# Batch 0 of a windowed attention with FFN: exponentials as weights, outputs turned by TensorE, parts of 372 and 396 queries

## The chip, the cores and the metric

One core of a Trainium2 chip runs one launch. The metric is the device time of that launch in microseconds; three runs of the kernel before gave 254.47, 255.00 and 255.22, median 255.0. The engines have short names in what follows: PE is TensorE, DVE is VectorE, ACT is ScalarE, POOL is GpSimd and SP is SyncE. SP, ACT and POOL can issue transfers (DMA); POOL's are the ones that change the type on the way.

## The reference

Attention over 4 batches of 8 heads, 768 positions, 64 channels per head. A query sees the last 128 positions up to itself, and the first four positions ("sinks") always. Its output, laid out as 3072 tokens by 512 channels, goes through an FFN whose gate is a ReLU, with 1536 inner channels.

```python
keep = is_sink | in_window                    # key < 4, or 0 <= query - key < 128
scores = where(keep, q @ k.T / sqrt(64), -1e9)
a = exp(scores - max(scores)); a = a / (sum(a) + 1e-9)
x = (a @ v) as (batch * seq, head * dim)
out = (maximum(x @ w_gate, 0) * (x @ w_val)) @ w_out
```

## The kernel before, in words

**Units.** Attention is done in 16 units of two heads each: unit i is head pair i % 4 of batch i // 4. For a unit, keys lie in a tile `kE` and queries in `qT`, both turned so that the channels are on the partitions (two heads on 128), with extra key tiles in `kE` that begin with copies of the four sinks. Sg computes a group of score tiles on PE into one of two PSUM pairs (`PP`), and ACT takes exponentials from there into `ee`. DVE multiplies masks in; for two groups of batch 0 the mask is added on PE beforehand, as a bias.

**Two ways from exponentials to the FFN's input.** For batch 0, V multiplies `ee` by `v` with queries along the columns, so that the output is already turned: a sum over ones gives the denominators, spread over 64 partitions, DVE turns them, takes reciprocals and turns them back (R), and one more DVE instruction writes `xT`. It runs in two parts of 384 queries. For batches 1 to 3, W takes slices of 128 columns of `ee` as weights and streams 65 columns of `v`, whose last column is 1 and gives the denominators; queries then lie on partitions in seven tiles (`QSEG`), and DVE normalises them into `xn`. For batch 1, X turns `xn` on PE and ACT copies the result into `xT`; for batches 2 and 3 the turn goes through DRAM.

**FFN.** `chunk(b, g, m)` is column tile m (128 inner channels, 12 of them) of half g of batch b's queries: four matmuls with `wg`, a ReLU on ACT, four matmuls with `wv`, and a product on DVE into `hT`. In PSUM it rotates through three of four banks G; the fourth is for turns and for output tiles. `ffn2` multiplies `hT` by `wo` and stores 128 rows per tile.

**Order.** The program is written out by hand. After a head that brings up the first half of batch 0, 96 slots follow, one chunk each: 24 for a batch, for batch 0 first its twelve tiles of g = 0, then those of g = 1. `prep[s]` is what is emitted ahead of the chunk of slot s (loads, casts and stores, mostly on SP and POOL), and `plan[s]` what comes after it on PE: H and T turn halves and wholes of k and q, S is a score group, V, W and X are as above, F an output matmul. From slot 24 on three output matmuls follow each slot; those left over come at the end.

**Queues.** Each engine takes its instructions in the order emitted. On SP: loads of k, q and v, stores and turns by transfer, and the output. On POOL: casts from float32 (k and q into `kn` and `qn`, v into `vn`) and between them the issues of the weight loads, `load_w`, for two column tiles at a time, 256 KB each for `wg` and `wv`. In the kernel before, `prep[1]` holds them in this order:

```python
prep[1] += [("half", 6), ("half", 7), ("w", 6, 8), ("v", 0, 3), ("v", 0, 4), ("w", 8, 10), ("v", 0, 5),
            ("v", 0, 6), ("w", 10, 12)]
```

`setup3` fills the ends of `ee` and the ones beside v, on POOL; it stands in `prep[7]`. `gate(u)` is a small write by ACT into a load's buffer; the loads of units 4 to 6, in `prep[8]`, follow it, and so they start when ACT gets there. The loads of `v` for batch 0 use row tiles 0 to 2 in the head and 3 to 6 after it.

Of the kernel before, what the change touches and what calls it, by code (L numbers as in the profile page):

```python
# [15 lines left out]
CUT = 384  # L16


@with_exitstack
def kernel(  # L20
# [12 lines left out]
    nc = tc.nc  # L33
# [8 lines left out]
    NR, PR = 12, 64  # L42
# [4 lines left out]
    npool = ctx.enter_context(tc.tile_pool(name="np", bufs=2))  # L47
# [22 lines left out]
    ones = const.tile([128, 64], BF16, name="ones")  # L70
# [4 lines left out]
    m0 = const.tile([128, 512], BF16, name="m0")  # L75
# [12 lines left out]

# [3 lines left out]
           3: (1, 0, 152, [(244, 244, 0, 140), (ODD + 136, 372, 140, 152)]),  # L92
           4: (1, 152, 507, [(244, 384, 152, 267), (ODD + 136, 384, 267, 507)]),
           5: (0, 0, 499, [(0, 0, 0, 247), (ODD, 120, 247, 499)])}

    VLAST = [(4, 2, 0, 252, 112), (6, 2, 252, 272, 364), (5, 2, 272, 416, 240), (4, 2, 416, 419, 364)]
    VSEG = [[(0, 0, 0, 247, 0), (1, 0, 247, 499, 120), (2, 1, 0, 140, 244), (3, 1, 140, 152, 372)],
            [(2, 1, 152, 267, 0), (3, 1, 267, 507, 0)] + VLAST]
# [5 lines left out]

    class Unit:
# [4 lines left out]

    def load_kq(u):
        for x, dst in ((k, kf[u.i % NQ]), (q, qf[u.i % NQ])):
            nc.sync.dma_start(out=dst[:], in_=x[u.b, 2 * u.p:2 * u.p + 2].rearrange("h (p n) d -> (h p) (n d)", n=NR))
# [31 lines left out]
    def cast_kq(u):  # L145
        for src, dst in ((kf[u.i % NQ], kn[u.i % 2]), (qf[u.i % NQ], qn[u.i % 2])):
            nc.gpsimd.tensor_copy(dst[:], src[:])

# [23 lines left out]

    def load_rows(u):
        for x, dst in ((q, qf), (k, kf)):
            nc.sync.dma_start(out=dst[u.i % NQ][:].rearrange("p (h e) -> p h e", h=2),
                              in_=x[u.b, 2 * u.p:2 * u.p + 2].rearrange("h (p n) d -> p h (n d)", n=6))

    def cast_rows(u):
        for src, dst in ((qf, qn), (kf, kn)):
            nc.gpsimd.tensor_copy(dst[u.i % 2][:].rearrange("p (n h d) -> p h n d", n=6, h=2),  # L180
                                  src[u.i % NQ][:].rearrange("p (h n d) -> p h n d", n=6, h=2))

    def to_dram(u):
        for i, x in enumerate((qn, kn)):
            nc.sync.dma_start(out=kqd[u.i - ND][i * S:i * S + S, :].rearrange("(p n) c -> p (n c)", n=6),
                              in_=x[u.i % 2][:])
# [15 lines left out]
    def load_w(m0, m1):  # L202
        for w, dst in ((moe_w_gate, wg), (moe_w_val, wv)):
            nc.gpsimd.dma_start(out=dst[:, :, m0 * 128:m1 * 128],
                                in_=w.rearrange("(ko ki) n -> ki ko n", ki=128)[:, :, m0 * 128:m1 * 128])
# [5 lines left out]
    def setup():  # L211
# [9 lines left out]
        nc.gpsimd.affine_select(out=m0[:, 0:247], in_=band[:, 0:247], compare_op=Alu.is_ge, fill=0.0,  # L221
                                base=119, pattern=[[0, 247]], channel_multiplier=-1)
        cp, ms = nc.vector.tensor_copy, nc.vector.memset
        for i in range(NT):
            ms(kE[i][:, 384:1176], 0.0)
        ms(ones[:], 1.0)
        ms(vn[0][:, 3, :, 0:64], 0.0)
        ms(vf[:, 6, :, :], 0.0)
        cp(m0[:, 247:499], band[:, 4:256])
        ms(m0[0:4, 247:499], 1.0)  # L230
        ms(m0[0:4, 0:120], 1.0)
        ms(m0[0:4, 120:247], 0.0)
        bias(mb[:, 0, 0:499], m0[:, 0:499])
        bias(mb[:, 1, 0:140], band[:, 0:140])
        bias(mb[:, 1, 140:152], band[:, 4:16])
        ms(mb[0:4, 1, 140:152], 0.0)
# [4 lines left out]
    def setup2(g):  # L241
        cp, ms = nc.vector.tensor_copy, nc.vector.memset
        if g == 0:
            cp(msk[:, 0, 8:252], m0[:, 0:244])
            cp(msk[:, 0, 252:504], m0[:, 247:499])
            cp(msk[:, 0, 504:507], m0[:, 244:247])
            return
# [8 lines left out]
    rot, srot = [0], [0]  # L256
    head = [True]
# [4 lines left out]

    def two():
        if head[0]:
            srot[0] += 2
            return G[srot[0] % 4][:], G[(srot[0] + 1) % 4][:]
        x = pair()
        return x[:, 0, :], x[:, 1, :]
# [6 lines left out]
    def T(u):  # L275
        t = u.i % NT
        tk, tq = G[3][:], pair()[:, 0, :]
        for x, ps in ((kn[u.i % 2], tk), (qn[u.i % 2], tq)):
            for n in range(NR):
                for h in range(2):  # L280
                    r = slice(64 * h, 64 * h + 64)
                    nc.tensor.transpose(ps.bitcast(BF16)[r, 64 * n:64 * n + 64], x[r, 64 * n:64 * n + 64], ident[r, r])
        vk, vq = (ps.bitcast(BF16)[:, 0:S].rearrange("d (n p) -> d p n", p=PR) for ps in (tk, tq))
# [3 lines left out]
        nc.vector.tensor_copy(to(qT[t]), vq)  # L287
        odd_tiles(u, nc.vector.tensor_copy)

    def T_half(c):  # L290
        t, x = c % NP, c // NP
        if c < 2:
            tk, tq = two()
        elif head[0]:
            both = pair()
            tk, tq = both[:, 0, :], both[:, 1, :]
        else:
            tk, tq = G[3][:, 0:256], G[3][:, 256:512]
# [15 lines left out]
    def Sg(u, s):  # L314
        t, bias = u.i % NT, u.b == 0 and s in (0, 3)
        g, b0, n, segs = SEG[5 if u.b == 0 and s == 0 else s]
# [12 lines left out]
        if s == 4:  # L329
            parts = [(152, 267, band[:, 140:255]), (267, 507, msk[:, 1, 264:504])]  # L330
        else:
            parts = [] if bias else [(b0, n, msk[:, g, b0:n])]
        for c0, c1, m in parts:
            x = ee[u.i % NE][:, g, :, c0:c1]
            nc.vector.tensor_tensor(x, x, m.unsqueeze(1).to_broadcast([128, 2, c1 - c0]), op=Alu.mult)  # L335
# [3 lines left out]
    def sums(u, part, out, w):  # L339
        segs = VSEG[part]  # L340
        for i, (j, g, c0, c1, o0) in enumerate(segs):
            for h in range(2):
                nc.tensor.matmul(out=out[64 * h:64 * h + 64, o0:o0 + c1 - c0], lhsT=w(j, h),  # L343
                                 rhs=ee[u.i % NE][:, g, h, c0:c1], start=i == 0, stop=i == len(segs) - 1,
                                 skip_group_check=True)

    def V1(u, part):

        pv, pd = two()
        sums(u, part, pd, lambda j, h: ones[:])  # L350
        return u, part, pv, pd

    def V2(u, part, pv, pd):

        R = npool.tile([128, CUT], F32, name="R")
        r = npool.tile([128, CUT // 32], F32, name="r")
        nc.vector.transpose(out=R[:], in_=pd[:, 0:CUT])
        nc.vector.reciprocal(r[:], R[:].rearrange("p (c e) -> p c e", e=32)[:, :, 0])
        nc.vector.transpose(out=R[:].rearrange("p (c e) -> p c e", e=32),
                            in_=r[:].unsqueeze(2).to_broadcast([128, CUT // 32, 32]))  # L360
        return u, part, pv, R

    def V3(u, part, pv):
        sums(u, part, pv, lambda j, h: vn[u.b % 2][:, j, 2 * u.p + h, 0:64])

    def V4(u, part, pv, R):
        nc.vector.tensor_tensor(xT[u.b % 2][:, u.p, CUT * part:CUT * part + CUT], pv[:, 0:CUT], R[:], op=Alu.mult)  # L367
        ready[u.b, u.p, part] = True

    def V(u, part):  # L370
        x = V1(u, part)
        V3(*x[:3])
        V4(*V2(*x))

    def setup3():
        for i in range(2):
            nc.gpsimd.memset(vn[i][:, :, :, 64:66], 1.0)
        for i in range(NE):
            nc.gpsimd.memset(ee[i][:, 0:2, :, 507:640], 0.0)
            nc.gpsimd.memset(ee[i][:, 2, :, 419:640], 0.0)  # L380

    def W(u):

        ps = pair()
        for h in range(2):
            for t, segs in enumerate(QSEG):
                for i, (j, g, c0) in enumerate(segs):
                    nc.tensor.matmul(out=ps[:, h, 65 * t:65 * t + 65], lhsT=ee[u.i % NE][:, g, h, c0:c0 + 128],  # L388
                                     rhs=vn[u.b % 2][:, j, 2 * u.p + h, 0:65], start=t == 0 and i == 0,
                                     stop=t == 6 and i == len(segs) - 1, skip_group_check=True)  # L390
        o = ps[:, :, 0:455].rearrange("p h (t e) -> p h t e", e=65)
        x, r = xn[u.i % 2], rn[u.i % 2]
        nc.vector.reciprocal(r[:], o[:, :, :, 64])
        nc.vector.tensor_tensor(x[:].rearrange("p t (h d) -> p h t d", h=2), o[:, :, :, 0:64],  # L394
                                r[:].unsqueeze(3).to_broadcast([128, 2, 7, 64]), op=Alu.mult)

    def X(u):

        ps = (G[3][:] if u.p < 2 else pair()[:, 0, :]).bitcast(BF16)
        c = 0  # L400
        for t in range(7):
            nc.tensor.transpose(ps[:, c:c + 128], xn[u.i % 2][:, t, :], ident[:])
            c += 128 - t % 2 * 4
        nc.scalar.copy(xT[u.b % 2][:, u.p, :], ps[:, 8:8 + S])
        for x in range(2):
            ready[u.b, u.p, x] = True
# [3 lines left out]
    def chunk(b, g, m):  # L410
        assert all((b, p, g) in ready for p in range(NP)), (b, g)
        x, h = xT[b % 2], hT[b % 2]
        c = slice(CUT * g, CUT * g + CUT)
# [30 lines left out]
    with tc.manual_schedule():  # L444
# [9 lines left out]
        for c in range(3, 6):  # L454
            load_half(c)
# [201 lines left out]
```

The softmax here doesn't subtract the row's maximum and nothing guards it: scores larger than these inputs give would overflow.

## Time and profile before

| | |
|---|---|
| median of the runs | 255.0 us |
| the profiled execution | 253.84 us |
| its span (first to last instruction) | 252.1 us |
| PE busy | 241.7 us |
| DVE, ACT, POOL busy | 131.6, 117.1, 69.6 us |
| first chunk begins | 20.78 us |
| its value half begins | 21.43 us |
| T of unit 4 begins (end of slot 11) | 44.37 us |
| slot 24 begins | 76.91 us |
| last output matmul begins after | 248 us |
| moved by DMA | 40.09 MB |

Times within the span count from its first instruction. A group's duration is from an instruction's start to its end, and matmuls overlap; what one costs PE is the distance between starts: 0.65 us for four matmuls of 384 columns, 0.216 for one of 512, 0.030 for one of W. Granted clock was full throughout by the profile.

### The profile page before, as it was taken

What the parts mean: (1) busy time and instruction counts of PE and PEld (TensorE: products, weight loads), DVE (VectorE), ACT (ScalarE), POOL (GpSimd) and SP (SyncE); (2) the same over time, 40 slices, a digit from 0 to 9 for tenths busy, and PEclk for the clock granted to TensorE, in tenths of its full rate; (3) what the DMA queues carried; (4) which work ended last, traced back from release to release, by engine and by line L of the source; (5) the groups of instructions that cost most, each with busy time, mean ns of one, the idle gap of its engine ahead of it and who ended that gap; (6) DMA issues with size and microseconds to landing.
All of it is one profiled execution on the core that took longest, in us unless ns stands there. A gap on an engine that the chain in (4) does not pass through costs nothing.

```text
span 252.1 us, 5608 instructions
## 1 busy us (share of the span) xinstructions
PE 241.7 (96%) x2219; PEld 140.1 (56%) x2219; DVE 131.6 (52%) x249; ACT 117.1 (46%) x215; POOL 69.6 (28%) x118
## 2 busy tenths in 40 slices
PE   7879999997999999999999999999999999999993
PEld 2445566665775556666555556666555555555441
DVE  7488888999882646754225555734232223222000
ACT  3656942695854654641436664532233332333121
POOL 6695593788133235502004600000000000000000
PEclk9999999999999999999999999999999999999999
DMA  7999999999999899989799511433211101111132
GB/s 190 271 264 195 193 171 316 291 248 279 268 247 212 218 225 330 302 206 211 160 212 241 118 42 37 111 99 77 76 44 43 42 0 44 43 42 44 51 116 83
DMA packets 75570, 40.09 MB, mean 159 GB/s; under 512 B 53528, under 2 KB 71448, under 8 KB 75544
## 3 DMA queue, kind: packets, MB, share of 16 engines
q1 hardware_dynamic: 67080, 34.62, 53.6%
q0 software_dynamic: 7920, 4.72, 13.1%
q8 instruction: 17, 0.28, 0.5%
q10 hardware_dynamic: 544, 0.39, 0.5%
q14 instruction: 9, 0.07, 0.1%
HBM read 28.48 MB, written 11.25 MB: 158 GB/s over the span
## 4 chain that ended last, share of the span: by engine, by line
PE 82%; DVE 7%; ACT 4%; DMA 2%; issue 2%; POOL 0%; SPq 0%; ACTq 0%; POOLq 0%; DVEq 0%
PE g L417 22%; PE g L422 22%; PE g L437 21%; PE pp L324 5%; PE pp L388 4%; PE pp L437 3%; ACT ee L328 3%; DMA kf<-in_k_dram 1%; DMA vf<-in_v_dram 1%; DVE hT L424 1%; DVE KQ L199 1%; PE pp L343 1%; PE g L343 1%; PE g L301 1%; PE pp L320 1%
## 5 line engine op out<-in xcount | busy, mean ns | idle before, releaser
L424 DVE TENSOR_TENSOR hT<-gs,g 128x384 bf16<-128x384 f32 x96 | 52.9, 552 | 79.3 <-PE g L422 78.3
L420 ACT ACTIVATE gs<-g 128x384 f32<-128x384 f32 x96 | 47.5, 495 | 81.4 <-PE g L417 78.3
L417 PE MATMUL g<-xT,wg 128*128 128x384 bf16 x384 | 78.3, 326 | 0.2 <-DVE xT L367 0.2
L422 PE MATMUL g<-xT,wv 128*128 128x384 bf16 x384 | 78.1, 326 | 0.0
L437 PE MATMUL g<-wo,hT 128*128 128x512 bf16 x252 | 66.7, 379 | 0.3 <-ACT ot L441 0.2
L417 PEld LDWEIGHTS <-wg 128*128 128x128 bf16 x384 | 36.0, 98 | 31.5 <-issue 0.5
L328 ACT ACTIVATE ee<-pp 128x998 bf16<-128x998 f32 (+4 forms) x52 | 44.6, 905 | 15.4 <-PE pp L324 15.3
L422 PEld LDWEIGHTS <-wv 128*128 128x128 bf16 x384 | 37.4, 98 | 25.3 <-DMA wv<-in_moe_w_val_dram 0.9
L437 PEld LDWEIGHTS <-hT 128*128 128x128 bf16 x288 | 26.6, 98 | 25.2 <-issue 0.7
L335 DVE TENSOR_TENSOR ee<-ee,msk 128x838 bf16<-128x838 bf16 (+3 forms) x44 | 31.1, 713 | 12.3 <-ACT ee L328 11.7
L143 POOL CAST vn<-vf 128x512 bf16<-128x512 f32 x28 | 19.8, 715 | 43.2 <-DMA vf<-in_v_dram 43.2
L441 ACT COPY ot<-g 128x512 f32<-128x512 f32 x21 | 12.3, 587 | 19.0 <-PE g L437 19.0
L324 PE MATMUL pp<-KQ 64*128 64x252 bf16 (+7 forms) x320 | 16.7, 223 | 2.3 <-DVE xn L394 1.5
L324 PEld LDWEIGHTS <-KQ 64*128 64x128 bf16 x320 | 10.7, 94 | 12.0 <-issue 8.7
L388 PEld LDWEIGHTS <-ee 128*128 128x128 bf16 x384 | 13.2, 97 | 1.6
L388 PE MATMUL pp<-vn,ee 128*128 128x65 bf16 x384 | 13.5, 193 | 0.0
L394 DVE TENSOR_TENSOR xn<-pp,rn 128x896 bf16<-128x896 f32 x12 | 13.1, 1091 | 0.4
L180 POOL CAST qn<-qf 128x768 bf16<-128x768 f32 x8 | 7.0, 872 | 18.5 <-DMA kqd<-qn 14.2
L180 POOL CAST kn<-kf 128x768 bf16<-128x768 f32 x8 | 7.2, 895 | 3.6 <-DMA kf<-in_k_dram 3.2
L437 PE MATMUL pp<-wo,hT 128*128 128x512 bf16 x36 | 8.1, 379 | 0.0
L273 PE MATMUL g<-idle 128*128 128x512 bf16 x15 | 5.7, 530 | 1.3 <-DVE warm L212 1.3
L308 ACT COPY KQ<-g 128x384 bf16<-128x384 bf16 (+3 forms) x15 | 3.9, 347 | 2.4 <-PE g L301 2.3
(90 smaller groups left out, 136.4 us busy)
## 6 DMA issues: line engine op xcount, KB each, us to landing
out_dram<-ot SPq DMA_DIRECT2D x24, 256.0 KB
kf<-in_k_dram SPq DMA_DIRECT2D x12, 384.0 KB
qf<-in_q_dram SPq DMA_DIRECT2D x12, 384.0 KB
vf<-in_v_dram SPq DMA_DIRECT2D x12, 256.0 KB
vf<-in_v_dram SPq DMA_DIRECT2D x12, 224.0 KB
kf<-in_k_dram SPq DMA_DIRECT2D x8, 192.0 KB
wg<-in_moe_w_gate_dram POOLq DMA_DIRECT2D x6, 256.0 KB, 8.0
wv<-in_moe_w_val_dram POOLq DMA_DIRECT2D x6, 256.0 KB, 9.1
```

The source lines that it names most:

```text
L143: copy(vn[b % 2][0:rows, j, :, 0:64], vf[0:rows, j, :, :])
L180: nc.gpsimd.tensor_copy(dst[u.i % 2][:].rearrange("p (n h d) -> p h n d", n=6, h=2), src[u.i % NQ][:].rearrange("p (h n d) -> p h n d", n= ...
L324: nc.tensor.matmul(out=ps[:, h, c0:c1], lhsT=kE[t][64 * h:64 * h + 64, x0:x0 + 128], rhs=qT[t][64 * h:64 * h + 64, q0:q0 + c1 - c0], start ...
L328: nc.scalar.activation(x, ps[:, :, b0:n], Act.Exp, bias=0.0, scale=scale)
L335: nc.vector.tensor_tensor(x, x, m.unsqueeze(1).to_broadcast([128, 2, c1 - c0]), op=Alu.mult)
L388: nc.tensor.matmul(out=ps[:, h, 65 * t:65 * t + 65], lhsT=ee[u.i % NE][:, g, h, c0:c0 + 128], rhs=vn[u.b % 2][:, j, 2 * u.p + h, 0:65], st ...
L394: nc.vector.tensor_tensor(x[:].rearrange("p t (h d) -> p h t d", h=2), o[:, :, :, 0:64], r[:].unsqueeze(3).to_broadcast([128, 2, 7, 64]), ...
L417: nc.tensor.matmul(out=gp[:, 0:CUT], lhsT=wg[:, ko, m * 128:(m + 1) * 128], rhs=x[:, ko, c], start=ko == 0, stop=ko == KO - 1)
L420: nc.scalar.activation(gs[:], gp[:, 0:CUT], Act.Relu, bias=0.0, scale=1.0)
L422: nc.tensor.matmul(out=vp[:, 0:CUT], lhsT=wv[:, ko, m * 128:(m + 1) * 128], rhs=x[:, ko, c], start=ko == 0, stop=ko == KO - 1)
L424: nc.vector.tensor_tensor(h[:, m, c], gs[:], vp[:, 0:CUT], op=Alu.mult)
L437: nc.tensor.matmul(out=op, lhsT=hT[b % 2][:, m, t * 128:(t + 1) * 128], rhs=wo[:, m, :], start=m == 0, stop=m == FM - 1)
```

## The change

Batch 0 takes the same way as batch 1, in two parts. Part 0 is `QSEG` tiles 0 to 2, queries 0 to 371; part 1 is tiles 3 to 6, queries 372 to 767. So chunks of batch 0 have 372 and 396 columns. V, R and the ones go; W and X take a part, and in the head a PSUM bank. X of part 0 is copied by DVE for the first two units and by ACT for the others; X of part 1 by ACT, all through one bank.

Slots of batch 0 come in two runs: tiles 0 to 8 of g = 0, tiles 0 to 8 of g = 1, then tiles 9 to 11 of each. Part 1 is wanted at slot 9 instead of 12; W of part 1 stands in slots 6 to 8 and X of part 1 in slots 7 and 8.

The head has a new order: four halves of k and q are loaded before v, the scores of unit 3 stand between W of units 0 and 1, one half moves into slot 0, and seven idle matmuls go. Weights `wg` for tiles 0 and 1 are issued after the third cast, `wv` after the casts of v. `prep[1]` and later entries change: `setup3` stands ahead of the v casts, tiles 8 and 9 follow the last of them, tiles 10 and 11 are issued in `prep[10]`, the loads of units 4 to 6 in `prep[7]`.

Units 4 to 7 are loaded by rows of 1536 bytes and turned by 12 matmuls of 128x128 instead of 48 of 64x64; for units 4 and 5 ACT copies q too. W0 to W3 of batch 1 move by one or two slots, 13 output matmuls instead of 6 stand in slot 23, and the very last output tile is done as two halves of 256 columns on two banks, copied by ACT and DVE and stored from SP and ACT.

```diff
@@ setup and geometry
+CUT0 = 372
+    PART = {0: (range(3), 0, CUT0), 1: (range(3, 7), CUT0, S), None: (range(7), 0, S)}
-           3: (1, 0, 152, [(244, 244, 0, 140), (ODD + 136, 372, 140, 152)]),
-           4: (1, 152, 507, [(244, 384, 152, 267), (ODD + 136, 384, 267, 507)]),
+           3: (1, 0, 128, [(244, 244, 0, 128)]),
+           4: (1, 128, 507, [(244, 372, 128, 252), (ODD + 136, 372, 252, 504), (244, 496, 504, 507)])}
@@ T, for units 4 to 7
             for n in range(NR):
-                for h in range(2):
-                    r = slice(64 * h, 64 * h + 64)
-                    nc.tensor.transpose(ps.bitcast(BF16)[r, 64 * n:64 * n + 64], x[r, 64 * n:64 * n + 64], ident[r, r])
+                c = slice(128 * n, 128 * n + 128)
+                nc.tensor.transpose(ps.bitcast(BF16)[:, c], x[:, c], ident[:])
...
-        nc.vector.tensor_copy(to(qT[t]), vq)
+        (nc.scalar.copy if u.p < 2 else nc.vector.tensor_copy)(to(qT[t]), vq)
@@ W and X by parts (V, V1 to V4 and sums are removed)
+    def W(u, part=None, bank=None):
+        tiles = PART[part][0]
+        n, w = len(tiles), 65 * len(tiles)
...
+        for h in range(2):
+            for t in tiles:
+                c = 65 * (t - tiles[0])
+                for i, (j, g, c0) in enumerate(QSEG[t]):
+                    nc.tensor.matmul(out=at[h][:, c:c + 65], lhsT=ee[u.i % NE][:, g, h, c0:c0 + 128],
+                                     rhs=vn[u.b % 2][:, j, 2 * u.p + h, 0:65],
...
+        nc.vector.reciprocal(r, o[:, :, :, 64])
+        nc.vector.tensor_tensor(x.rearrange("p t (h d) -> p h t d", h=2), o[:, :, :, 0:64],
+                                r.unsqueeze(3).to_broadcast([128, 2, n, 64]), op=Alu.mult)
+    def X(u, part=None, bank=None, copy=nc.scalar.copy):
+        if bank is None:
+            bank = G[3][:] if u.b == 0 or u.p < 2 else pair()[:, 0, :]
...
+        copy(xT[u.b % 2][:, u.p, q0:q1], ps[:, c:c + q1 - q0])
@@ the last output tile
+        if b == B - 1 and t == 5:
+            if m == 0:
+                for x, bank in enumerate((op, OP[1][opn[0] % 3 - 1])):
+                    c = slice(d_model // 2 * x, d_model // 2 * x + d_model // 2)
...
+                    (nc.scalar.copy, nc.vector.tensor_copy)[x](ot[:, c], bank[:, 0:d_model // 2])
+                    (nc.sync, nc.scalar)[x].dma_start(out=out[b * S + t * 128:b * S + (t + 1) * 128, c], in_=ot[:, c])
@@ the head, new (the old one is in the listing above)
+        for c in range(4):
+            load_half(c, (nc.sync, nc.scalar))
+        for j in range(3):
+            load_v(0, j)
...
+        cast_half(2)
+        T_half(2, (g[2], g[3]))
+        load_w(0, 2, (0,))
...
+        cast_half(3)
+        T_half(3, (g[0], g[1]))
+        for j in range(3):
+            cast_v(0, j)
+        load_w(0, 2, (1,))
+        load_w(2, 4)
+        Sg(U[2], 0)
+        Sg(U[2], 3)
+        W(U[0], 0, g[2])
+        Sg(U[3], 0)
+        W(U[1], 0, g[0])
+        X(U[0], 0, g[3], nc.vector.tensor_copy)
+        Sg(U[3], 3)
+        W(U[2], 0, g[2])
+        X(U[1], 0, g[1], nc.vector.tensor_copy)
+        W(U[3], 0, g[0])
+        X(U[2], 0, g[3])
+        X(U[3], 0, g[1])
@@ the slots
+        for b, runs in enumerate((((0, 9), (9, FM)),) + ((((0, FM),),) * (B - 1))):
+            slots += [(b, g, m) for m0, m1 in runs for g in range(2) for m in range(m0, m1)]
-        for s, w in {0: "H1 S04 S02", 1: "H2 S14", 2: "H3 S12", 3: "S24 S22", 4: "S34 S32", 6: "V01", 7: "V11",
-                     9: "V21", 10: "V31"}.items():
+        for s, w in {0: "H0", 1: "S04 H1", 2: "S02 H2 S14", 3: "S12 H3", 4: "S24 S22", 5: "S34 S32", 6: "W01",
+                     7: "W11 X01 W21", 8: "X11 W31 X21 X31"}.items():
-        for s, w in {11: "T0", 12: "T1", 13: "S00 S01", 14: "S02 S10", 15: "T2 S11", 16: "S12 T3", 17: "W0 S20",
-                     18: "S21 S22", 19: "W1 S30 X0", 20: "S31 S32", 21: "W2 X1", 22: "W3 X2", 23: "X3"}.items():
+        for s, w in {11: "T0", 12: "T1", 13: "S00 S01", 14: "S02 S10", 15: "T2 S11", 16: "S12 T3", 17: "S20 S21",
+                     18: "S22 W0", 19: "S30 X0", 20: "S31 W1", 21: "S32 X1", 22: "W2", 23: "W3 X2 F8 X3 F5"}.items():
-        prep[1] += [("half", 6), ("half", 7), ("w", 6, 8), ("v", 0, 3), ("v", 0, 4), ("w", 8, 10), ("v", 0, 5),
-                    ("v", 0, 6), ("w", 10, 12)]
-        prep[7] += [("setup3",)]
-        prep[8] += [("load", 4), ("load", 5), ("load", 6)]
+        prep[1] += [("half", 6), ("half", 7), ("w", 6, 8), ("setup3",), ("v", 0, 3), ("v", 0, 4), ("v", 0, 5), ("v", 0, 6),
+                    ("w", 8, 10)]
+        prep[7] += [("load", 4), ("load", 5), ("load", 6)]
-        prep[10] += [("kq", 5)]
-        prep[11] += [("setup2", 0)]
+        prep[10] += [("kq", 5), ("w", 10, 12)]
```

## The prediction

> **What bounds the kernel now.** I read the page's busy shares and slices first, then the stretches, then the waits, then the timeline where two queues meet.
>
> ```profile
> PE 241.7 (96%) x2219; PEld 140.1 (56%) x2219; DVE 131.6 (52%) x249; ACT 117.1 (46%) x215; POOL 69.6 (28%) x118
> ...
> PE   7879999997999999999999999999999999999993
> ...
> DMA  7999999999999899989799511433211101111132
> ```
>
> TensorE is busy nearly everywhere, so removed matmuls count, but the DMA row is just as full up to two thirds of the first half. There are two clocks in this kernel until about 100 us: PE's work and the transfers. The stretches show the second one (columns: us; busy us of PE, PEld, DVE, ACT, POOL; granted clock; DMA share; GB/s):
>
> ```profile
> 15.00:31.00 16.00, 14.95 (x158) 8.80 (x158) 13.29 (x31) 12.04 (x30) 10.22 (x18) 1.00 1.37 202
> 31.00:37.00 6.00, 6.00 (x81) 3.96 (x78) 5.04 (x12) 3.15 (x8) 6.00 (x13) 1.00 1.30 172
> 37.00:54.00 17.00, 16.57 (x278) 10.58 (x275) 15.98 (x33) 8.92 (x14) 10.30 (x14) 1.00 1.03 279
> ...
> 58.00:73.00 15.00, 13.51 (x210) 9.80 (x208) 13.47 (x21) 9.52 (x15) 6.04 (x7) 1.00 1.14 264
> ```
>
> A share over 1 means that the 16 engines had work all the time. From 31 to 37 only weights ran (172 GB/s); the loads of units 4 to 7 began when they were through. The waits, whole span:
>
> ```profile
> POOL vn L143 <- DMA vf<-in_v_dram: 43.2, 21, 19.5
> ...
> PE pp L324 <- DVE xn L394: 1.5, 1, 1.5
> ...
> PEld L422 <- DMA wv<-in_moe_w_val_dram: 0.9, 3, 0.4
> ```
>
> PE hardly waits; its one long wait (1.5 us) is for W's normalisation on DVE. The three short waits for `wv` matter more than their size: the value halves of column tiles 0, 2 and 4 start the moment their weights land (21.43, 25.72 and 30.02 us), so weights arrive with no margin. POOL, which issues those loads, meanwhile waits for `v`. Its timeline, then PE at column tile 8, then how long a `wv` load took from issue to landing:
>
> ```profile
> 26.10 0.75 POOL L204 DMA_DIRECT2D wg<-in_moe_w_gate_dram  x1
> 26.83 0.75 POOL L204 DMA_DIRECT2D wv<-in_moe_w_val_dram  x1
> 29.91 0.72 POOL L143 CAST vn<-vf 128x512 bf16<-128x512 f32 x1 [2.33 <-DMA vf<-in_v_dram]
> 30.92 0.95 POOL L143 CAST vn<-vf 128x512 bf16<-128x512 f32 x1 [0.28 <-DMA vf<-in_v_dram]
> 31.82 0.74 POOL L204 DMA_DIRECT2D wg<-in_moe_w_gate_dram  x1
> 32.55 0.75 POOL L204 DMA_DIRECT2D wv<-in_moe_w_val_dram  x1
> ```
> ```profile
> 37.10 0.82 PE L417 MATMUL g<-xT,wg 128*128 128x384 bf16 x4
> 37.76 0.81 PE L422 MATMUL g<-xT,wv 128*128 128x384 bf16 x4
> ```
> ```profile
> DMA to landing us min/median/max: 5.7/9.1/12.2
> ```
>
> The pair for tiles 8 and 9 is issued at 26.1, ahead of the last two `v` casts; the pair issued at 31.8, behind them, is the one for tiles 10 and 11. That last pair is the quickest (5.7 us for `wv`, landed at 38.2), because it ran alone.
>
> **What the Trainium skill says.** "DMA: Bandwidth & Descriptors", section Queues, rings and completion order: each engine takes turns between its queues, packet by packet. The trace agrees: from 59 to 72 us the packet records show 107 `wo` packets and 101 load packets a us. Same page, SWDGE pipeline (Anatomy of one DMA): about 2 us fixed; here the pair issued at 31.8 has its first packets at 34.0. "TensorE: Matmul & The Clock Gate", Part 1: the array runs at half clock until some 3.4 us of activity, and falls back after an idle window; here the first seven idle matmuls take 0.43 us each, the six at 19.15 take 0.22. The same page's opening table: engines other than PE take their instructions strictly in order; POOL's row above, waiting for `v` with weights behind it, is that.
>
> **The change, step by step.** Durations are from the profiled execution (span 252.1, 253.8 with what lies around it; the median of the runs, 255.0, is 1.2 above, and I add the sum to the median).
>
> *Head.* Gone: the sums over ones, R's transposes (0.58 each), one half (moved to slot 0) and seven of fifteen idle matmuls. New: W and X in parts. Walk: the fourth k/q half now precedes `v`, so v2 is cast at about 12.4 (it ended 11.7 before); exp of unit 2 ends 13.8 by ACT's sum (four half copies 0.95 each, exps 1.0 + 0.4); unit 3's exps 14.4 to 15.95. Then DVE is last: W0 to W3 at recip 0.25 + multiply 0.5 (estimate between L367's 0.55 and the 384/896 share of L394's 1.09), two X copies at 0.5, W3 done 18.2; X3 0.2, copy 0.45: the last xT at 19.0. Gate half of chunk 0 then; its value half needs wv(0,2), now issued behind the v casts at 12.45 (12.95 before), landing about 19.5. Against 21.43 before: -1.9, bounds -2.3 and 0 (idle gaps of 0.7 to 1.2 us without the six warming matmuls could leave half clock: up to 1.7).
>
> *Slots 0 to 7.* H0 adds 0.43. V's 0.88 + 0.10 for the switch of array shape becomes W 20 x 0.030 + X 4 x 0.056 = 0.83. From the value half of slot 0 at 19.5 to chunk 8: 0.65 + 7 chunks at 1.30, four H 1.7, eight S 2.1, switches of shape 0.6, W01, W11, X01 and W21 2.0, a wait for wv(2,4) of 0.4 (it lands near 23.9): 36.1; with what a walk misses, 36.4.
>
> *Chunk 8: the new wait.* POOL's list is now w(6,8), eight memsets, v casts 3 to 6, then w(8,10). What has crossed by then (all k/q halves, all v, weights up to tile 7) is the same in both kernels, and before it was across at 30.9, with no gap in the queues. So v6's cast again stands at about 30.9 and w(8,10) is issued at about 31.8: 5.7 us later than before, with first packets at 34.0. The engines idle 3 us. Worse, slot 7's gate now comes at about 33.3 instead of 36.1, so the loads of units 4 to 6 run from 34.4 against it. Alone 512-byte weight packets went at 361 a us, 1536-byte loads at 230; taking turns that is 1/(1/361 + 1/230) = 141 a us, say 150, as shares summed to 1.08 in the earlier overlap. wg has 512 packets: 140 by 34.4, the rest by 36.9; wv by 40.3; landing 1.2 later, 38.1 and 41.5. PE waits 1.7 before the gate half and 2.7 before the value half; both the chunk's evictions and every later slot queue behind it. Value half at 41.5 against 37.76: **+3.75**. Bounds: 38.2 (no contention, +0.4) and 43.5 (+5.7).
>
> *Slots 8 to 11.* X11, W31, X21, X31 now stand directly before chunk 9. From the value half: 0.65, X11 0.22, W31 0.60, DVE 1.0 (hT first), X31 0.22, copy 0.55; three of the next gate's four matmuls need not wait: 2.25, then three chunks of 396 at 1.34. 6.9 against 6.6: +0.3.
>
> *Slots 12 to 23.* T: 48 small transposes (0.88 + 0.10) become 12 of 128x128 (12 x 0.056): -0.3 x 4 = -1.2. Chunks of 396: +0.2. Waits before: 0.6 at 48.9, 0.2 near 58.5, 1.5 at 61.5, together 2.3; with W0 moved to slot 18 and T0's, T1's q on ACT I expect new ones, S10 behind a fuller ACT 0.4, S21 behind T3's q copy 0.5, X0 behind W0's DVE work 0.6: -0.8. Seven more output matmuls of 0.216 in slot 23: +1.5, taken back at the end.
>
> *Later.* Slots 24 on are unchanged. S of units 8 to 11 wait some 0.5 us for late data before; with PE later and the transfers only about 2 us behind (the idle 3 us less a gap of 0.7 at 40 to 42 that fills), these go: -0.5. Tail: -1.5 for the moved matmuls, and the last tile in halves: copy 0.59 to 0.33, store half as long: -0.4.
>
> Sum: +3.75 + 0.3 - 1.2 + 0.2 - 0.8 + 1.5 - 0.5 - 1.9 = **+1.35**; 255.0 + 1.35 = **256.4 us**. (The head's -1.9 is inside the anchor at chunk 8, where the wait swallows it.)
>
> **The rivals.** *Faster (0.22).* The weights for tile 8 are there when PE comes. It takes a v6 cast some 1.5 us earlier, or loads of units 4 to 6 that start after 37. Then the value half runs at 37.4 and the sum is -0.35 + 0.3 - 1.2 + 0.2 - 0.8 + 1.5 - 1.9 = -2.25: 252.8. For it: alone, the pair would land 3.3 us sooner than I say; against: POOL's order is fixed, and the queues were full until 30.9. It decides at a landing of 37.4; each us later costs one.
> *Transfers decide later (0.20).* Chunk 8 waits little, but the engines' idle 3 us come back at units 8 to 11, whose S had no slack (the sinks of unit 10 end at 95.05, PE starts at 95.11). Lag 1.8 to 2.6 less the 1.9 of the tail: 255.0 to 255.7; I take 255.3.
> *Slower still (0.15).* Half clock in slots 0 to 2, or wv at 43.5: 258.3.
> *The forecast's mechanism (0.43)*: 256.4, own range 255.3 to 257.6.
>
> **How the numbers follow.** A measurement of this kernel can tell about 0.3%, 0.77 us. The forecast's case lies nine tenths above 255.77, the transfers' case a quarter, the worst case wholly: 0.39 + 0.05 + 0.15 = 0.59 slower; same 0.18; faster 0.23. The range reaches down to 252.6, which leaves out a bit under half of the faster case, and up to 258.8.
>
> **What would show it.** Right: after, POOL's timeline has w(8,10) behind the last v cast near 32, and PE idles 2.5 us or more before L361 of slot 8, put down to `wv`; the DMA has a hole near 31 to 34; first chunk about 1.5 us earlier; T pieces 0.68; no 1.5 us wait at the S after W0. Wrong: w(8,10) landed before PE came, or PE already late in slots 0 to 4 (half clock or wv(0,2)), or a DVE chain before chunk 9 longer than 2.5 us.

## The result: 282.3 us, and the profile after

The kernel after takes 282.33 us (median of four runs, 278.90 to 286.93), against 254.74 for the kernel before. The ratio is 1.100, with a 95% interval of 1.092 to 1.108. Some executions of a kernel take longer than the others, so ratios and differences between kernels are taken from those within 1.5% of the kernel's fastest, whose median stands in square brackets behind the median of all: 282.33 [279.97] us for after, 254.74 [254.74] for before. The prediction was 256.4 us and a range of 252.6 to 258.8: the direction was right, the size wrong by a factor of some 20. The profiled execution of after took 286.93 us, at a mean clock of 0.974. So single durations are taken from it, and a total only from slot 24 on, where its granted clock is full (1.00 from 94 to 246 us, as in the traces of before, of both edits and of the runs with 12 and with 7 output matmuls below).

The first view is the same as before: busy shares, PE's slices, the granted clock and the DMA's slices.

```profile
PE 244.7 (86%) x2063; PEld 141.4 (50%) x2084; DVE 120.9 (42%) x227; ACT 120.8 (42%) x222; POOL 67.9 (24%) x120
...
PE   7869825997899978879889988978998988988895
...
PEclk9999985899799999999999999999999999999999
DMA  7999599799999834599997410231411000010113
```

PE's busy time is only 3 us longer than before (241.7); idle time was added. It stands in two places. One is a hole in slices 6 and 7, the second of them at half clock. The other is spread: before, PE's digits from slice 11 on were 9 but for the last; here they lie between 7 and 9 up to the last. The stretches that answer to those of before (columns: us; busy us of PE, PEld, DVE, ACT, POOL; granted clock; DMA share; GB/s):

```profile
15.00:31.00 16.00, 13.45 (x149) 7.99 (x147) 10.96 (x25) 11.12 (x28) 10.64 (x24) 1.00 1.31 199
31.00:37.00 6.00, 4.89 (x77) 3.47 (x77) 4.52 (x9) 3.08 (x9) 3.19 (x5) 1.00 0.45 137
37.00:54.00 17.00, 8.05 (x75) 5.03 (x73) 3.57 (x8) 2.93 (x6) 4.50 (x6) 0.70 1.10 249
58.00:73.00 15.00, 12.58 (x131) 7.89 (x130) 13.74 (x22) 12.04 (x18) 12.23 (x17) 0.97 1.11 255
```

From 31 to 37 us the DMA share is 0.45 where it was 1.30. From 37 to 54 PE works 8.05 us where it worked 16.57, at a mean clock of 0.70. The waits (engine, line, what it waited for: us in total, times, longest):

```profile
POOL vn L134 <- DMA vf<-in_v_dram: 44.4, 13, 18.7
PE g L388 <- ACT ot L392: 17.3, 20, 1.7
...
PE g L356 <- DMA wg<-in_moe_w_gate_dram: 6.1, 1, 6.1
...
PE g L361 <- DMA wv<-in_moe_w_val_dram: 4.2, 4, 2.1
...
PE pp L290 <- DVE KQ L259: 2.3, 1, 2.3
```

The largest is new: output matmuls (L388) waited 20 times for ACT's copy of an output tile (L392), 17.3 us in all. The kernel before has the same pair of lines once, with 0.2 us. The others are the weights of chunk 8 (6.1 for `wg`, 2.1 of the 4.2 for `wv`) and S21 behind T3's q copy. POOL's list, then PE at column tile 8, then the time from issue to landing of `wv`:

```profile
32.91 1.53 POOL L134 CAST vn<-vf 128x512 bf16<-128x512 f32 x2 [3.78 <-DMA vf<-in_v_dram]
34.39 0.74 POOL L190 DMA_DIRECT2D wg<-in_moe_w_gate_dram  x1
35.12 0.75 POOL L190 DMA_DIRECT2D wv<-in_moe_w_val_dram  x1
```
```profile
36.94 0.77 PE L321 MATMUL pp<-vn,ee 128*128 128x65 bf16 x20
43.84 1.42 PE L356 MATMUL g<-xT,wg 128*128 128x372 bf16 x4 [6.13 <-DMA wg<-in_moe_w_gate_dram]
47.41 1.42 PE L361 MATMUL g<-xT,wv 128*128 128x372 bf16 x4 [2.15 <-DMA wv<-in_moe_w_val_dram]
```
```profile
DMA to landing us min/median/max: 6.9/10.2/12.2
```

The pair for tiles 8 and 9 is issued last, as foretold, but at 34.4 and not at 31.8, and `wv` takes the longest of all, 12.2 us. The value half starts at 47.41, where before it was 37.76. The matmuls then last 1.42 us a group in place of 0.8: half clock.

One of the 20 waits for `ot`, on PE and then on ACT:

```profile
101.09 0.61 PE L290 MATMUL pp<-KQ 64*128 64x252 bf16 x14
101.64 0.60 PE L388 MATMUL g<-wo,hT 128*128 128x512 bf16 x2
103.84 0.38 PE L388 MATMUL g<-wo,hT 128*128 128x512 bf16 x1 [1.60 <-ACT ot L392]
```
```profile
101.55 1.76 ACT L294 ACTIVATE ee<-pp 128x838 bf16<-128x838 f32 x2 [0.51 <-PE pp L290]
103.19 0.59 ACT L392 COPY ot<-g 128x512 f32<-128x512 f32 x1
```

A slot's three output matmuls are split into two and one. The two end an output tile, the one begins the next, in the same PSUM bank. So it cannot start until ACT has copied the bank, 0.59 us, and here the copy also stands behind two exponentials. Where no score group comes just before, the idle time is 0.67 us each (16 of the 20); behind exponentials it is 1.6 to 1.7.

### The profile page after: what moved, and what is told of

It reads as the page before. It is cut to its first block, busy times and chain, and to the rows that moved or that the text cites. A ratio compares the mean times of both kernels' runs of the same rounds, so it can differ in the third digit from the quotient of the medians.

```text
span 285.0 us, 5299 instructions
## 1 busy us (share of the span) xinstructions
PE 244.7 (86%) x2063; PEld 141.4 (50%) x2084; DVE 120.9 (42%) x227; ACT 120.8 (42%) x222; POOL 67.9 (24%) x120
## 4 chain that ended last, share of the span: by engine, by line
PE 67%; DMA 13%; ACT 7%; SPq 5%; DVE 4%; issue 3%; POOL 1%; ACTq 0%; POOLq 0%; DVEq 0%
PE g L361 19%; PE g L388 19%; PE g L356 18%; DMA vf<-in_v_dram 5%; DMA wv<-in_moe_w_val_dram 4%; ACT ot L392 4%; PE pp L321 4%; DMA qf<-in_q_dram 4%; PE pp L290 3%; SPq L131 3%; ACT ee L294 3%; PE pp L388 2%; DVE xn L327 1%; DVE ee L296 1%; SPq L113 1%
## 5 line engine op out<-in xcount | busy, mean ns | idle before, releaser
L363 DVE TENSOR_TENSOR hT<-gs,g 128x384 bf16<-128x384 f32 (+2 forms) x96 | 53.0, 552 | 116.7 <-PE g L361 112.9
L359 ACT ACTIVATE gs<-g 128x384 f32<-128x384 f32 (+2 forms) x96 | 47.6, 496 | 109.5 <-PE g L356 108.7
L356 PE MATMUL g<-xT,wg 128*128 128x384 bf16 (+2 forms) x384 | 79.7, 330 | 6.3 <-DMA wg<-in_moe_w_gate_dram 6.1
L361 PE MATMUL g<-xT,wv 128*128 128x384 bf16 (+2 forms) x384 | 79.4, 330 | 4.2 <-DMA wv<-in_moe_w_val_dram 4.2
L388 PE MATMUL g<-wo,hT 128*128 128x512 bf16 x232 | 65.6, 379 | 18.8 <-ACT ot L392 17.3
L388 PEld LDWEIGHTS <-hT 128*128 128x128 bf16 x276 | 25.4, 98 | 24.6 <-issue 1.9
L166 POOL CAST kn<-kf 128x768 bf16<-128x768 f32 x12 | 10.7, 890 | 43.3 <-DMA kqd<-kn 15.5
L321 PEld LDWEIGHTS <-ee 128*128 128x128 bf16 x512 | 18.4, 99 | 3.3 <-issue 1.4
L290 PE MATMUL pp<-KQ 64*128 64x252 bf16 (+6 forms) x328 | 17.3, 225 | 2.4 <-DVE KQ L259 2.3
L392 ACT COPY ot<-g 128x512 f32<-128x512 f32 x21 | 12.3, 587 | 14.8 <-PE g L388 14.1
L321 PE MATMUL pp<-vn,ee 128*128 128x65 bf16 x464 | 17.3, 195 | 0.6 <-POOL vn L134 0.6
L327 DVE TENSOR_TENSOR xn<-pp,rn 128x896 bf16<-128x896 f32 (+1 forms) x16 | 15.9, 991 | 0.5
L341 ACT COPY xT<-g 128x396 bf16<-128x396 bf16 (+2 forms) x8 | 4.5, 560 | 8.0 <-PE g L338 8.0
```

The source lines that it names most:

```text
L290: nc.tensor.matmul(out=ps[:, h, c0:c1], lhsT=kE[t][64 * h:64 * h + 64, x0:x0 + 128], rhs=qT[t][64 * h:64 * h + 64, q0:q0 + c1 - c0], start ...
L321: nc.tensor.matmul(out=at[h][:, c:c + 65], lhsT=ee[u.i % NE][:, g, h, c0:c0 + 128], rhs=vn[u.b % 2][:, j, 2 * u.p + h, 0:65], start=c == 0 ...
L327: nc.vector.tensor_tensor(x.rearrange("p t (h d) -> p h t d", h=2), o[:, :, :, 0:64], r.unsqueeze(3).to_broadcast([128, 2, n, 64]), op=Alu ...
L356: nc.tensor.matmul(out=gp[:, 0:n], lhsT=wg[:, ko, m * 128:(m + 1) * 128], rhs=x[:, ko, c], start=ko == 0, stop=ko == KO - 1)
L359: nc.scalar.activation(gs[:, 0:n], gp[:, 0:n], Act.Relu, bias=0.0, scale=1.0)
L361: nc.tensor.matmul(out=vp[:, 0:n], lhsT=wv[:, ko, m * 128:(m + 1) * 128], rhs=x[:, ko, c], start=ko == 0, stop=ko == KO - 1)
```

## The experiments

Each run was timed beside the kernel before on the same chip; a ratio is to that. "Both edits" below means the first and third of these experiments together.

**12 output matmuls in slot 23 in place of 13.**

```diff
-... 22: "W2", 23: "W3 X2 F8 X3 F5"}.items():
+... 22: "W2", 23: "W3 X2 F7 X3 F5"}.items():
```

> The kernel after, with 12 output matmuls in slot 23 in place of 13 (7 ahead of X3, 5 behind it), so that an output tile again ends with a slot. Theory (phase): with 13, each tile's first matmul follows the last one of the tile before inside a triple, in the same PSUM bank, and waits for ACT's copy; with 12 a chunk lies between. The waits of L388 for ot fall from 17.3 us to under 1, and the time falls by 15 to 18 us, to 263 to 266. Rival (late weights and the clock): the slots from 24 on are slow because the stall at chunk 8 left the clock or the transfers behind; moving one matmul changes under 2 us.

Measured: 260.42 [257.45] us (ratio 1.012, interval 1.006 to 1.019), 22.5 us less than after. The row of the output matmuls, which ended `18.8 <-ACT ot L392 17.3` in after, now reads:

```profile
L388 PE MATMUL g<-wo,hT 128*128 128x512 bf16 x220 | 61.3, 379 | 1.4 <-issue 0.2
```

The wait for `ot` is gone from the list. In the two profiled executions slot 24 begins at 93.19 and 92.06, and from there to the last matmul after takes 188.1 us, this kernel 169.4. One matmul fewer, moved to the end, is worth 18.7 us there. The phase theory holds. The times gave more, 22.5 us where 15 to 18 was expected; where the rest of it comes from stays open.

**The kernel before, with 7 in place of 6.**

```diff
-        plan[23].append(("F", 6, 0))
+        plan[23].append(("F", 7, 0))
```

> The kernel before, with 7 output matmuls in slot 23 in place of 6; nothing else. Theory (phase): 7 leaves the remainder 1 when divided by 3, as 13 does, so each later tile's first matmul waits for the copy; some 20 tile changes by 0.85 us, 17 us more: 270 to 273. Rival (the waits belong to the new kernel's late transfers): one more matmul early and one fewer at the end, within 1 us of 254.7.

Measured: 273.44 [273.45] us (ratio 1.074, 1.069 to 1.079), 18.8 us slower than before. The wait is there, which before was next to nothing (before first, then this run):

```profile
PE g L437 <- ACT ot L441: 0.2, 1, 0.2
```
```profile
PE g L437 <- ACT ot L441: 15.9, 18, 1.7
```

So one output matmul more is enough, in a kernel with nothing else of the change. An output tile is 12 matmuls and a slot takes three: 6 and 12 leave tile ends at slot ends, with a chunk's 1.3 us of matmuls over each copy; 7 and 13 leave them inside a slot. One tile end of the kernel before, on PE and then on ACT: the copy begins at 91.96, while the next chunk runs, and the next output matmul at 92.61.

```profile
90.40 0.82 PE L437 MATMUL g<-wo,hT 128*128 128x512 bf16 x3
91.06 0.81 PE L417 MATMUL g<-xT,wg 128*128 128x384 bf16 x4
91.71 0.81 PE L422 MATMUL g<-xT,wv 128*128 128x384 bf16 x4
92.61 0.81 PE L437 MATMUL g<-wo,hT 128*128 128x512 bf16 x3
```
```profile
91.96 0.59 ACT L441 COPY ot<-g 128x512 f32<-128x512 f32 x1
```

**The weights of tiles 8 and 9 early again.**

```diff
-... ("setup3",), ("v", 0, 3), ("v", 0, 4), ("v", 0, 5), ("v", 0, 6), ("w", 8, 10)]
+... ("setup3",), ("v", 0, 3), ("v", 0, 4), ("w", 8, 10), ("v", 0, 5), ("v", 0, 6)]
```

> The kernel after, with the weights of tiles 8 and 9 issued behind the cast of v tile 4, as before, in place of behind that of v tile 6. Theory (late weights): the value half of chunk 8 runs at about 37.5 to 38.5 in place of 47.41, TensorE keeps full clock there, and 8 to 10 us go: 270 to 274. The waits for ot stay at about 17. Rival (the transfers are too many whatever the order): the value half stays later than 42 and under 5 us go.

Measured: 273.98 [273.98] us (ratio 1.077), 6.0 less than after. The value half of chunk 8 starts at 38.28 without a wait, the clock there is full, and the wait for `ot` is 17.3 us again:

```profile
38.28 0.79 PE L361 MATMUL g<-xT,wv 128*128 128x372 bf16 x4
```

The theory holds in place; in size it gives less than the 8 to 10 us expected.

**Both edits.**

> The kernel after with both edits: 12 output matmuls in slot 23, and the weights of tiles 8 and 9 behind v tile 4. If the two causes are the whole loss and are independent, they add: about 26 us less than after, 253 to 257, level with the kernel before within 1%. If a third cause is left (half clock elsewhere, the loads of units 4 to 7, the new order of W and S in slots 17 to 23) it stays above 258.

Measured: 255.76 [255.23] us, ratio 1.0014 (0.9991 to 1.0037). Both causes together are the loss: 24.7 of 25.2 us. With the phase in order the late weights cost 257.45 - 255.23 = 2.2 us (two runs against 13), less than the 6.0 that they cost beside the wrong phase. Both are under the 9.65 us by which chunk 8 is late in the profiled execution of after; how late it is in the other runs, no trace shows.

**In the kernel before, the same weights late.**

```diff
-... ("w", 6, 8), ("v", 0, 3), ("v", 0, 4), ("w", 8, 10), ("v", 0, 5), ("v", 0, 6), ("w", 10, 12)]
+... ("w", 6, 8), ("v", 0, 3), ("v", 0, 4), ("v", 0, 5), ("v", 0, 6), ("w", 8, 10), ("w", 10, 12)]
```

> The kernel before, with only this changed: the weights of tiles 8 and 9 are issued behind the cast of v tile 6 and not behind that of v tile 4. Theory (the place in POOL's list alone makes the stall): the issue moves from 26 to about 32, the value half of slot 8 from 37.76 to 44 to 47, and the time rises by 6 to 10 us, to 261 to 265. Rival (the stall needs the new kernel's earlier arrival and its earlier loads of units 4 to 6): those loads start in slot 8, behind the stall itself, so the weights land by 39 and the time rises by under 3 us.

Measured: 255.02 [254.99] us (ratio 1.003, 1.000 to 1.006). My theory fell and the rival held. The issue moves to 32.79, near what I had expected, but the value half of slot 8 comes at 38.45 and waits only this:

```profile
38.45 0.82 PE L422 MATMUL g<-xT,wv 128*128 128x384 bf16 x4 [0.46 <-DMA wv<-in_moe_w_val_dram]
```

There ACT lets the loads of units 4 to 6 go at 36.1 us, and by the packet records their first packet moves at 40.4, when tiles 8 and 9 are across. In after they are let go at 33.2, SP issues the first at 33.48, before POOL comes to the weights at 34.39, and their packets run from 34.5; those of the weights begin at 37.9 and then take turns with them, at about 100 to 165 a us each, where weights alone go at 350 to 370. In this kernel the late issue by itself does not hurt; in after the loads run ahead of it.

**The loads of units 4 to 6 later, in slot 9 and in slot 8**, each in the kernel with 12 output matmuls:

```diff
-        prep[7] += [("load", 4), ("load", 5), ("load", 6)]
-        prep[9] += [("kq", 4), ("load", 7), ("lv", 1)]
+        prep[9] += [("load", 4), ("load", 5), ("load", 6), ("kq", 4), ("load", 7), ("lv", 1)]
```

> The kernel of the run with 12 output matmuls in slot 23, with the loads of units 4 to 6 in slot 9 in place of slot 7; the weights of tiles 8 and 9 still come last. It prices the contention between these loads and the weights. The prediction's sum: contention costs the weights 3.3 us (41.5 against 38.2), so here the value half of chunk 8 comes at 44, from 47.4. Rival (the weights land late because they are issued late and cross slowly by themselves): it stays at 46 or later. The time may rise all the same, since units 4 to 6 now come later for T.

```diff
-        prep[7] += [("load", 4), ("load", 5), ("load", 6)]
+        prep[8] += [("load", 4), ("load", 5), ("load", 6)]
```

> The kernel of the run with 12 output matmuls in slot 23, with the loads of units 4 to 6 in slot 8, as before the change, in place of slot 7; the weights of tiles 8 and 9 still come last. Theory (the late issue hurts only when these loads run against it): the gates are then behind slot 7's ReLU, some 2.7 us later, the value half of chunk 8 comes at 39 to 41 and T of units 4 and 5 hardly waits; the time is 255.5 to 257.5, level with the run with both edits. Rival (the late issue costs by itself): it stays at 259 or more, as with the loads in slot 7 (260.4) or 9 (264.2).

Measured: 264.21 [264.21] us in slot 9 (ratio 1.042, 1.035 to 1.049) and 259.91 [259.90] in slot 8 (1.024, 1.018 to 1.030), against 260.42 [257.45] in slot 7 (1.012). Chunk 8 in these two, slot 9 first:

```profile
38.34 0.80 PE L356 MATMUL g<-xT,wg 128*128 128x372 bf16 x4 [0.33 <-DMA wg<-in_moe_w_gate_dram]
39.80 0.80 PE L361 MATMUL g<-xT,wv 128*128 128x372 bf16 x4 [0.66 <-DMA wv<-in_moe_w_val_dram]
```
```profile
40.68 0.80 PE L361 MATMUL g<-xT,wv 128*128 128x372 bf16 x4 [1.36 <-DMA wv<-in_moe_w_val_dram]
```

Without the loads beside them the weights, issued at 34.49, let the value half go at 39.80, against 46.96 in the kernel it was derived from: contention cost 7.2 us there, more than the 3.3 that I had put down for it and expected to find. Of this, about 2 us are a later first packet (3.5 us from issue in after, 1.4 in slot 9's run); the rest is the slower crossing. Yet nothing is won in the time. With slot 9 the DMA engines have almost nothing to move from 31 to 37 (share 0.24, 32 GB/s) and by the packet records nothing from 40 to 44; T of unit 4 then waits 1.5 us for its casts, T of unit 5 1.05, and slot 12 begins at 49.45, where it was 47.38 with both edits. Later X0 waits 2.80 us for DVE, and S of a unit of batch 2 2.24 us. With slot 8 (the loads are let go at 38.5) the lag returns at S of a unit of batch 2, behind the sinks that POOL writes after the unit's turn by transfer:

```profile
102.27 0.53 PE L290 MATMUL pp<-KQ 64*128 64x252 bf16 x10 [2.43 <-POOL KQ L181]
```

So of slot 8's two expectations the place of the value half was right (39 to 41) and the time was not (255.5 to 257.5): the rival's 259 or more came out, for a reason that it did not name. As these traces read, what the transfers lose in this stretch is paid at chunk 8, at T of units 4 and 5, or at units 8 to 11. That this is the whole of the time is not shown. With the weights issued in time (both edits) none of these waits is there.

**What is left: the stop at `wv` in chunk 0.** The kernel with both edits, with six idle matmuls between the halves of chunk 0:

```diff
+        if (b, g, m) == (0, 0, 0):
+            spin(6, 2)
         for ko in range(KO):
             nc.tensor.matmul(out=vp[:, 0:n], ...
```

> The kernel with both edits and, in addition, six idle matmuls (1.3 us at full clock) between the gate half and the value half of chunk 0, where TensorE stood 2.5 us for wv and then ran at half clock from 20.7 to 26.2. Theory (the stop takes the clock away): TensorE keeps full clock from 17 to 30, the mean clock is 0.995 or more, and 2 to 3 us go: 252.5 to 253.5. Rival (the half clock has another cause, or later waits take the gain): the time stays at 255.8 within 0.8.

Measured: 255.84 [255.84] us (ratio 1.007, 1.004 to 1.009). PE at chunk 0 with both edits alone, and then with the idle matmuls:

```profile
20.72 1.42 PE L361 MATMUL g<-xT,wv 128*128 128x372 bf16 x4 [2.54 <-DMA wv<-in_moe_w_val_dram]
21.93 0.53 PE L267 MATMUL g<-ident,kn 128*128 128x128 bf16 x3
```
```profile
20.82 0.80 PE L363 MATMUL g<-xT,wv 128*128 128x372 bf16 x4 [1.28 <-DMA wv<-in_moe_w_val_dram]
21.46 0.33 PE L267 MATMUL g<-ident,kn 128*128 128x128 bf16 x3
```

The clock is kept (1.42 becomes 0.80), and between the two profiled executions chunk 8 starts 1.8 us earlier. Two traces alone would not show that the idle matmuls did it: with q on ACT (next) PE stood 1.89 us at the same place without them and ran on at full clock. The mean clock of every run does: it was below 0.995 in 15 of 20 runs with both edits and in 12 of 20 with q on ACT, but in none of the 5 here and in 2 of 14 with both mends below. So the mechanism is shown. Its worth is not, since the time did not fall: the rival holds.

**The q copies of T2 and T3 on ACT.** With both edits, S21 in slot 17 stood 1.85 us. DVE and POOL there:

```profile
59.08 2.41 DVE L296 TENSOR_TENSOR ee<-ee,msk 128x838 bf16<-128x838 bf16 x1
61.41 0.94 DVE L259 COPY KQ<-pp 128x768 bf16<-128x768 bf16 x1
```
```profile
59.29 1.74 POOL L134 CAST vn<-vf 128x512 bf16<-128x512 f32 x3
60.96 1.21 POOL L166 CAST kn<-kf 128x768 bf16<-128x768 f32 x1
```

A mask product that takes 0.60 us elsewhere takes 2.41 while POOL casts without a break; in this trace all ten products of its shape that meet no work of POOL take 0.60. T3's q copy is behind it on DVE, and S21 needs the bank that this copy empties. The Trainium skill, "GPSIMD Engine Reference", section Specifications, says that GpSimd's SBUF interfaces are shared with VectorE, with contention for DVE instructions that have two SBUF inputs; the product is one of these, and the trace agrees.

```diff
-        (nc.scalar.copy if u.p < 2 else nc.vector.tensor_copy)(to(qT[t]), vq)
+        nc.scalar.copy(to(qT[t]), vq)
```

> The kernel with both edits and, in addition, the q copies of T2 and T3 on ACT in place of DVE. Theory (S21 in slot 17 waits 2.0 us for T3's q copy behind a mask product that took 2.41 us, and half clock follows): the wait at slot 17 falls under 0.5, no half clock follows, and 2.5 to 3.5 us go: 252.3 to 253.3. Rival (ACT is as late as DVE there): under 0.8 us.

Measured: 255.71 [255.14] us (ratio 1.002, 1.000 to 1.005). The wait at S21 falls to 0.28 us and the clock stays full in the profiled execution, but the time does not move: the rival's number, though ACT was not late. A part came back two slots later, where X0 waits 0.55 us for W0's normalisation; with both edits it did not wait there.

**Both of these together.**

> Both edits, the six idle matmuls in chunk 0, and the q copies of T2 and T3 on ACT. Each alone left the time at 255.8 and 255.7. If the two stops (1.3 to 2.5 us at wv, 1.9 at S21) each hide the other's gain, because a later stage only starts when transfers are there, together they give 252.5 to 253.8. Rival (what is left is TensorE's own work and the transfers): 254.5 to 256, again.

Measured: 255.29 [255.05] us (ratio 1.005, 1.002 to 1.008): the rival. In its profile S waits 1.80 us from 96.9 on, again behind POOL's sinks of a unit of batch 2.

**`wv` of tiles 0 and 1 ahead of the v casts**, with both edits and q on ACT:

```diff
+        load_w(0, 2, (1,))
         for j in range(3):
             cast_v(0, j)
-        load_w(0, 2, (1,))
```

> Both edits, the q copies of T2 and T3 on ACT, and wv for tiles 0 and 1 issued ahead of the three v casts of the head in place of behind them, some 2.8 us earlier. Theory (the head's wait for wv is the last large idle time): the value half of chunk 0 follows its gate half at 18.1 with no wait over 0.3, slot 24 begins 1.5 to 2.5 us earlier, 253 to 254. Rival (the bytes in the queues decide, and what is sent earlier delays the next weights and v): the wait comes back at chunks 2 to 6, and the time stays within 0.8 of 255.7.

Measured: 254.26 [254.19] us, ratio 0.9997 (0.9974 to 1.0021). The value half of chunk 0 starts at 18.28, against 21.43 before, but chunk 2 waits 1.35 us for its own `wv` and chunk 6 0.60. Slot 24 begins at 79.08, no earlier than with q on ACT alone (79.17): X0 stood 1.70 us. The waits came back where the rival said; the time lies between the two, above the theory's 253 to 254 and further below 255.7 than the rival's 0.8.

**X0 of batch 1 one slot later**, on top of that:

```diff
-... 19: "S30 X0", 20: "S31 W1", ...
+... 19: "S30", 20: "S31 X0 W1", ...
```

> The kernel of the run with wv first, with X0 of batch 1 in slot 20 behind S31 in place of slot 19 behind S30. There X0 waited 1.7 us for W0's normalisation on DVE. Theory (that stop is idle time on the path): no wait over 0.3 at X0, slot 24 begins at 77.5 to 78.5, the time is 252.6 to 253.6 and so under both kernels. Rival (the transfers of units 8 to 11 are the second clock and take the place of the stop: S of units 10 or 11 waits about 2 us for late copies): the time stays at 254.3 within 0.8.

Measured: 254.09 [253.68] us, beside 254.78 [254.67] for the kernel before; ratio 0.998 (0.995 to 1.001). Slot 24 begins at 77.15, 0.35 below what was expected, and the wait at X0 there is gone. S of batch 2 waits 0.66 us from 94.7 on, less than the rival's 2; the median of all is still the rival's. The time is not apart from that of the kernel before: no version here is shown to beat it. A lead, and no more since it was picked out afterwards: the 13 of its 22 runs with a mean clock of 0.995 or above have a median of 253.15, where 23 of 27 of the kernel before have 254.60. In its profile the waits for `wv` are these:

```profile
PEld L361 <- DMA wv<-in_moe_w_val_dram: 4.1, 3, 2.0
...
PE g L361 <- DMA wv<-in_moe_w_val_dram: 1.6, 1, 1.6
```

PE is still there before the weights.

## Why the prediction was wrong, step by step

**The step that failed** is the last of "Slots 12 to 23": seven more output matmuls in slot 23, "+1.5, taken back at the end". I costed them as work moved, and did not ask where in an output tile each later slot would then stop. Counting was enough: 12 matmuls a tile, three a slot, 13 at the start. The trace of before shows what covers the copy: a chunk's 1.3 us over a copy of 0.59, with 0.2 us of waiting in all. Of the signs that I had listed as right, the late pair of weights, the hole in the transfers and the T pieces all came; none of them looked at slots 24 on. It cost 17.3 us of waits in the trace and, against 12 matmuls, 18.7 us from slot 24 to the last matmul; the same edit in the old kernel cost 18.8. With the remainder in order the term is as I had it: from slot 24 to the last matmul the kernel with both edits takes 169.4 us against 171.0 before, 1.5 less. Without the failed step the kernel takes 260.42 [257.45] us, the second 1.1 above the 256.4 forecast; luck has a share in that, since two other terms missed, as follows.

**Chunk 8** was right in kind and mis-sized. I had POOL's order, the hole in the transfers (predicted from 31 to 34; by the packet records nothing crosses from 32.5 to 34.5), the wait for `wv` and the loads of units 4 to 6 against it. Two terms were off in the profiled execution: the v6 cast and so the issue, 34.4 in place of 31.8 (2.6 us), and contention, 7.2 us where I had 3.3 (3.9 us). 41.5 + 2.6 + 3.9 = 48.0, about the 47.41 measured, outside my bounds of 38.2 to 43.5. The clock came on top: I let it fall only in slots 0 to 2 of the rival "slower still", and it fell at this stop. In the times the whole step costs less than in that trace: 2.2 us with the phase in order and 6.0 without, where I had +3.75.

**Head**: the gate half of chunk 0 came at 17.61, 1.4 us before the walk's 19.0, and then waited 1.2 us for `wv`; the value half was expected at 19.5 and measured at 19.84. **Slots 0 to 7**: PE is at chunk 8 at 37.7 where I had 36.4. The head's gain is swallowed at chunk 8, as the sum had it; with both edits most of it goes at chunk 0 itself (2.54 us for `wv`, and half clock), with `wv` first at chunks 2 and 6 (1.35 and 0.60 us), so that chunk 8 begins there at 37.19, where it was 37.10 before the change.

**Slots 8 to 11**: from value half to T0 6.9 us expected; 7.1 with both edits, 8.5 in after, part of it at half clock.

**T**: 0.68 a turn expected, 0.67 measured. **Waits of slots 12 to 23**: I expected 0.8 us less. With both edits S21 alone waits 1.85 and half clock follows; with q on ACT, X0 takes it over (up to 1.70, where I had put 0.6). From T0 to slot 24, less the six further output matmuls (1.3 us), the kernel with both edits takes 34.2 us against 32.5 before: +1.7 in place of -1.8. In the last run above, with q on ACT and X0 later, it takes 31.1: -1.4, so it was above all the waits that I had wrong here, and not the work.

**Tail**: -0.4 for the halves; from the start of the last matmul to the end of the span it is 3.7 us in after against 4.3.

**The rivals.** "Faster" asked for weights in time: both edits make them so, and the time is 255.76 [255.23], not 252.8: the head's gain was lost at chunk 0, and slots 12 to 23 took more and not less. "Transfers decide later" did not decide in after, but in the profiled executions it is what took the gain of slot 8's loads and of the two mends together (S behind late sinks, 2.43 and 1.80 us). The rival that was missing is the one that happened: an output tile's end falling inside a slot.

## What to carry to other kernels

When work is dealt out in fixed portions, an edit that moves a few instructions of it changes the remainder: find where each later accumulation ends, and check that the copy out of its bank is still covered by work into another bank. When a load is moved behind others, ask which transfers are let go ahead of it; here the loads let go ahead set the price, more than the delay itself. And time saved at one wait is a gain only if the next resource, here the weights and then the units of batch 2, is early enough to use it.

## What the hardware showed that was not expected

The length of a stop of PE did not decide whether half clock followed. From the first chunk on, and chunk 8 aside, stops of 1.53 to 2.54 us were followed in nine places of the traces by 3.4 or 6.8 us at half clock (1.42 us for four matmuls of 372 columns in place of 0.80), while twenty others of 1.57 to 2.80 us were not, among them the long waits for `ot`; stops of up to 1.45 us never were. The weights for tiles 8 and 9 took 12.2 us to land with the loads of units 4 to 6 already issued and 4.5 us in the run that had those loads in slot 9. And DVE's product of two SBUF operands took 2.41 us in place of 0.60 while POOL made three casts in a row, and 3.21 in the run with `wv` first.
